# Fused attention and feed-forward kernel: the loads of seven token chunks, each cut into two transfers

## The chip, the cores and the metric

The kernel runs on one core of a Trainium2 chip. The metric is the device time of one execution in microseconds (us). The kernel before takes 298.97 us, the median of three runs (298.57, 298.97 and 299.29 us).

A core has TensorE (PE, matrix products, with a row PEld for its weight loads), VectorE (DVE), ScalarE (ACT), GpSimd (POOL) and SyncE (SP). They run side by side, each with its own queue of instructions, and wait for one another through semaphores. Sixteen DMA engines move data between the main memory (HBM) and the on-chip memory (SBUF). In this kernel POOL issues all loads but two, and SP issues the stores and the transposing DMAs.

## The reference, cut to what matters

```
q, k, v: (8 batches, 8 heads, 576 tokens, 64) float32; w_in (512, 2048), w_out (2048, 512)

scores = (q @ k.T) / sqrt(64)
Dmat   = gamma[h] ** (i - j) where i >= j, else 0      # gamma[h] = 1 - 2**(-5 - h)
x      = (scores * Dmat) @ v                           # heads side by side: (4608, 512)
h      = x @ w_in
out    = (h * tanh(softplus(h))) @ w_out               # (4608, 512) float32
```

## The kernel before, in words

The 4608 tokens are cut into 36 chunks of 128. Chunks 0 to 7 are the first 128 tokens of each batch. Then come, for each pair of batches, three chunks of each batch and one chunk that holds the last 64 tokens of both: chunks 8 to 10 and 11 to 13 belong to batches 0 and 1, chunk 14 is their shared rest, 15 to 17 and 18 to 20 belong to batches 2 and 3, 21 is their shared rest, and so on. Four chunks form a feed-forward tile, so there are nine tiles.

Attention is done chunk by chunk with a running state for each batch (`total`). For a chunk n from 8 on the steps are these:

- `load(n)` (line 267) issues the loads of q, k and v, each 128 tokens by 8 heads by 64, 256 KB, on POOL's queue (line 276). A shared chunk has two loads of 64 tokens for each of the three (line 283). q and k go to the halves of one buffer, `qkraw`, of which there are five; v goes to `vraw`, of which there are seven.
- `step_p(n)` scales q and k on DVE (`qks`, line 295), two instructions for a chunk. `step_v(n)` scales v (`vs`, line 302), on DVE up to chunk 19 and on POOL after it.
- `step_t(n)` transposes q and k: for chunks up to 15 on TensorE (line 316), from chunk 16 on by a transposing DMA that SP issues (line 324, `qkT`).
- `visit(n)` handles two chunks on TensorE: the states of the next pair (line 393), the outputs of this pair (lines 452 and 469) and the scores of the next pair (line 338). It ends with two copies out of PSUM to the transposed activations `xT` (line 481), one on ACT and one on DVE.

The feed-forward products (line 518; line 523 is the same in two halves) fill TensorE between the visits: `g1` writes to one of two PSUM banks called `hp` and ACT applies the activation (line 547), `g2` sums into `ops`, and line 599 copies the result out for the store. The two `xT` copies read the same two `hp` banks, so `g1` cannot go on in a bank before its copy is done.

The order of all work is written out by hand. The loads of chunks 8 to 11 are issued in a row (line 661). Those of chunks 12 to 16 are issued in the loop over u (line 708), and those of 17, 18 and 19 wait for an activation of the third tile (line 512, `gated`). From chunk 20 on `hold(n)` (line 485) comes first: a one-column copy on POOL that reads the transposed `qkT` of chunk n. POOL works in order, so the loads behind it are not issued before that transposing DMA has landed. `hold(16)` stands before the load of chunk 20, and `hold(18)` before that of chunk 21. `load_k0(b)` (line 257) loads 256 KB of k once more for the states.

In the trace the DMAs that POOL issues carry eight semaphores in turn, and each issue waits for the semaphore that it will use: it waits until the DMA issued eight before it on POOL's queue has landed. The code does not say this; the framework does it.

Of the kernel before, what the change touches and what calls it, by code (L numbers as in the profile page):

```python
# [16 lines left out]
def kernel(  # L17
# [18 lines left out]
    nc = tc.nc  # L36
    B, H, S, D = q.shape
    assert (B, H, S, D) == (8, 8, 576, 64)
    P = 128
# [227 lines left out]
    def load(n, gate=None):  # L267
        if n >= n_chunks:
            return
        b, c = chunks[n]  # L270
        qkr = io.tile([P, 2, H, D], F32, name="qkraw")
        vr = io.tile([P, H, D], F32, name="vraw", bufs=7)
        live[n] = {"qkr": qkr, "v": vr}
        for t, src in ((qkr[:, 0], q), (qkr[:, 1], k), (vr, v)):
            if c < 4:
                ins = nc.gpsimd.dma_start(  # L276
                    out=t, in_=src[b, :, ds(P * c, P), :].rearrange("h p d -> p h d"))
                if gate is not None:
                    behind(ins, gate)
                    gate = None  # L280
            else:
                for e in range(2):
                    nc.gpsimd.dma_start(
                        out=t[ds(64 * e, 64)],
                        in_=src[b + e, :, ds(512, 64), :].rearrange("h p d -> p h d"))
# [76 lines left out]
    def behind(ins, others):  # L362

        sync = mybir.DependencyInfo(mybir.DependencyClass.Sync, mybir.DependencyReason.DATA)
        tc.add_manual_dep(ins.ins, others.ins.name, sync, reason="row halves and a bank")
# [168 lines left out]
    def g1(t, f, parts=1, begun=None):  # L534
        if t not in gts:
            gts[t] = gp.tile([P, nF, NCH * P], BF16, name="gT")
        if begun is not None:
            hp = begun
        elif (t, f) == (0, 2):
            hp = ps_o.tile([P, NCH * P], F32, name="ops")  # L540
        else:
            hp = ps_h.tile([P, NCH * P], F32, name="hp")
        n = NCH * P // parts
        for j in range(0 if begun is None else 1, parts):
            for c in range(KC):
                product(hp[:, ts(j, n)], w_in_t[:, c, ts(f, P)], xts[t][:, c, ts(j, n)], c == 0, c == KC - 1)
        done = nc.scalar.activation(gts[t][:, f, :], hp, AX.Mish)  # L547
        if (t, f) in gated:
            load(gated[t, f], done)
            queued[0] += 1  # L550
# [110 lines left out]
    for b in range(4):  # L661
        load(N0 + b)
        if b == 0:
            load_k0(0)
# [13 lines left out]
    for i in range(nF):  # L678
        for step in steps.get(i, "").split():
            n = int(step[1])  # L680
# [17 lines left out]
    def more_loads(upto):  # L698
        for _ in range(2):
            if queued[0] <= upto:  # L700
                load(queued[0])
                queued[0] += 1
# [55 lines left out]
    for t in range(2, nT + 1):  # L758
        for i in range(nF):
            n, w = NCH * (t + 1) + i // 8 * 2, i % 8  # L760
# [104 lines left out]
```

## Time and profile before

| | |
|---|---|
| median of three runs | 298.97 us |
| the profiled execution's own time | 298.96 us |
| its span (first to last instruction) | 297.3 us |
| PE busy | 288.0 us (97%) |
| DVE, ACT, POOL busy | 136.7, 133.0, 128.5 us |
| moved by DMA | 47.97 MB, mean 161 GB/s |
| POOL's own DMA queue (q0) | 32.25 MB, 50.6% of the 16 engines' span |
| granted TensorE clock | 1.0 throughout |

The profile is that of one execution. An instruction's line gives its start, its duration, the engine, the line of the kernel, the operation, and what it writes and reads (out<-in). In brackets stands the time that the engine sat idle before it and who ended that wait. "To landing" is the time from the issue of a DMA to the moment when all its data are there. Times are counted from the start of the span.

### The profile page before, as it was taken

Reading aid. Unit: us, or ns where it says so; the run is one execution under the profiler, and the core shown is the slowest. Engines: PE = TensorE matmul, PEld = TensorE weight load, DVE = VectorE, ACT = ScalarE, POOL = GpSimd, SP = SyncE. Lnnn points to the kernel's source line nnn. Section 1 sums busy time; section 2 is a strip of 40 time slices with the busy share of each in tenths; the row PEclk is TensorE's granted clock in tenths of the full one; section 3 lists DMA queues with packets and bytes.
Section 4 is the critical chain, followed back from the end, with each engine's and each line's share of the span. In section 5 each row is a group of like instructions: output and inputs, shape, how many; then the busy total and the mean of one; then the engine's idle time right before and its main releaser. Section 6 shows DMA issues by size and latency. Waiting matters only on the chain.

```text
span 297.3 us, 7902 instructions
## 1 busy us (share of the span) xinstructions
PE 288.0 (97%) x3444; PEld 157.4 (53%) x3482; DVE 136.7 (46%) x241; ACT 133.0 (45%) x219; POOL 128.5 (43%) x170
## 2 busy tenths in 40 slices
PE   8999998999999999999999999999999999999996
PEld 3566886555556545456645454545454544444443
DVE  3841546598858727453546453535354222010011
ACT  5667225876656544434363435343444333433200
POOL 8845665767662279294658547283020000000000
PEclk9999999999999999999999999999999999999999
DMA  7999999999999979998989988685414110110131
GB/s 149 208 202 205 204 239 217 337 237 191 273 239 180 197 164 223 196 218 188 237 165 228 176 217 213 140 206 142 87 45 98 37 37 35 37 35 35 53 91 71
DMA packets 42259, 47.97 MB, mean 161 GB/s; under 512 B 23920, under 2 KB 31088, under 8 KB 42224
## 3 DMA queue, kind: packets, MB, share of 16 engines
q0 software_dynamic: 15424, 32.25, 50.6%
q1 hardware_dynamic: 26656, 15.01, 22.2%
q8 instruction: 27, 0.44, 0.6%
q10 hardware_dynamic: 144, 0.20, 0.2%
q14 instruction: 8, 0.07, 0.1%
HBM read 38.80 MB, written 9.44 MB: 162 GB/s over the span
## 4 chain that ended last, share of the span: by engine, by line
PE 81%; DMA 12%; POOL 3%; issue 2%; DVE 1%; POOLq 0%; DVEq 0%
PE hp L518 38%; PE ops L518 30%; DMA vpair<-in_v_dram 5%; DMA w_out_t<-in_moe_w_out_dram 4%; DMA w_in_t<-in_moe_w_in_dram 3%; PE hp L523 2%; PE ops L523 2%; PE sc L338 1%; PE sc L393 1%; PE hp L469 1%; PE hp L452 1%; PE hp L591 1%; POOL gT L107 1%; PE sc L316 1%; POOL gT L118 1%
## 5 line engine op out<-in xcount | busy, mean ns | idle before, releaser
L518 PE MATMUL hp<-xT,w_in_t 128*128 128x512 bf16 (+1 forms) x507 | 126.3, 376 | 1.3 <-DVE xT L249 0.6
L547 ACT ACTIVATE gT<-hp 128x512 bf16<-128x512 f32 x143 | 85.4, 598 | 93.0 <-PE hp L518 87.1
L518 PE MATMUL ops<-w_out_t,gT 128*128 128x512 bf16 x410 | 101.6, 379 | 2.0 <-issue 1.9
L518 PEld LDWEIGHTS <-w_in_t 128*128 128x128 bf16 x528 | 51.3, 98 | 54.1 <-issue 0.8
L518 PEld LDWEIGHTS <-gT 128*128 128x128 bf16 x478 | 45.5, 98 | 52.2
L599 DVE COPY res<-ops 128x512 f32<-128x512 f32 x28 | 19.3, 691 | 90.7 <-PE ops L518 90.7
L295 DVE TENSOR_TENSOR qks<-qkraw,gqk 128x512 bf16<-128x512 f32 x56 | 35.3, 685 | 5.3 <-DMA qkraw<-in_k_dram 5.3
L276 POOL DMA_DIRECT2D qkraw<-in_q_dram x24 | 21.7, 904 | 8.3 <-DMA vpair<-in_v_dram 2.7
L487 POOL COPY held<-qkT 128x1 bf16<-128x1 bf16 x10 | 2.6, 264 | 51.3 <-DMA qkT<-qks 51.3
L302 POOL TENSOR_TENSOR vs<-vraw,gv 128x512 bf16<-128x512 f32 x16 | 16.4, 1045 | 15.1 <-PE hp L452 15.0
L276 POOL DMA_DIRECT2D vraw<-in_v_dram x24 | 21.2, 884 | 2.7 <-DMA vpair<-in_v_dram 1.5
L276 POOL DMA_DIRECT2D qkraw<-in_k_dram x24 | 21.3, 888 | 1.7 <-DMA w_out_t<-in_moe_w_out_dram 1.0
L481 DVE CAST xT<-hp 128x512 bf16<-128x512 f32 x13 | 9.0, 691 | 25.8 <-PE hp L469 25.8
L481 ACT CAST xT<-hp 128x512 bf16<-128x512 f32 x14 | 8.2, 586 | 28.1 <-PE hp L469 28.1
L523 PEld LDWEIGHTS <-gT 128*128 128x128 bf16 x164 | 15.7, 98 | 3.2
L429 DVE TENSOR_TENSOR total<-sc,total 128x256 f32<-128x256 f32 x40 | 16.9, 422 | 1.0
L344 DVE TENSOR_TENSOR sm<-sc,mask 128x1024 bf16<-128x1024 f32 x14 | 17.0, 1216 | 0.7 <-PE sc L338 0.7
L523 PE MATMUL hp<-xT,w_in_t 128*128 128x256 bf16 x102 | 15.7, 273 | 0.0
L523 PEld LDWEIGHTS <-w_in_t 128*128 128x128 bf16 x104 | 10.2, 98 | 6.7
L432 ACT CAST ssb<-total 128x768 bf16<-128x768 f32 (+3 forms) x13 | 11.7, 897 | 1.7 <-DVE total L429 1.6
L518 PE MATMUL hp<-w_out_t,gT 128*128 128x512 bf16 x49 | 12.0, 379 | 0.2 <-issue 0.2
L523 PE MATMUL ops<-w_out_t,gT 128*128 128x256 bf16 x80 | 10.4, 273 | 0.2
(123 smaller groups left out, 250.4 us busy)
## 6 DMA issues: line engine op xcount, KB each, us to landing
out_dram<-res SPq DMA_DIRECT2D x31, 256.0 KB, 3.2
qkraw<-in_q_dram POOLq DMA_DIRECT2D x24, 256.0 KB, 6.3
qkraw<-in_k_dram POOLq DMA_DIRECT2D x24, 256.0 KB, 6.5
vraw<-in_v_dram POOLq DMA_DIRECT2D x24, 256.0 KB, 6.8
w_out_t<-in_moe_w_out_dram POOLq DMA_DIRECT2D x4, 512.0 KB, 11.9
k0r<-in_k_dram POOLq DMA_DIRECT2D x8, 256.0 KB, 7.5
gT<-in_k_dram POOLq DMA_DIRECT2D x8, 128.0 KB, 6.6
gT<-in_v_dram POOLq DMA_DIRECT2D x2, 512.0 KB, 7.2
```

Source lines behind the costliest of these rows:

```text
L107: nc.gpsimd.dma_start(out=fst[t][name][:, b, :], in_=(q, k)[i][4 * t + b, :, 0:P, :].rearrange("h (g r) d -> g h (r d)", r=8))
L276: ins = nc.gpsimd.dma_start(out=t, in_=src[b, :, ds(P * c, P), :].rearrange("h p d -> p h d"))
L295: nc.vector.tensor_tensor(slots[:, :, y], heads[:, :, y], factors[:, :, y].unsqueeze(3).to_broadcast([P, NP, 2, D]), op=OP.mult)
L302: engine.tensor_tensor(vs, live[n]["v"], gv[:, c, :].unsqueeze(2).to_broadcast([P, H, D]), op=OP.mult)
L344: nc.vector.tensor_tensor(sm.rearrange("p e x n i -> p (e x n) i"), live[n]["sc"].rearrange("p e x n i -> p (e x n) i"), mask.unsqueeze(1) ...
L429: nc.vector.tensor_tensor(new[:, k], st[:, j, x], total[b], op=OP.add)
L432: casts.append(lambda copy: copy(lows[:, 0:k], new[:, 0:k]))
L481: copy(xts[t][:, :, ds(P * s, 2 * P)].rearrange("p h (x j i) -> p j h x i", x=2, j=2)[:, j], both[j])
L518: newest[0] = nc.tensor.matmul(to, lhsT=w, rhs=x, start=first, stop=last)
L523: nc.tensor.matmul(to[:, ts(j, n)], lhsT=w, rhs=x[:, ts(j, n)], start=False, stop=False, skip_group_check=True)
L547: done = nc.scalar.activation(gts[t][:, f, :], hp, AX.Mish)
L599: copy(ot, ops)
```

## The change

Each load of q, k and v of chunks 10 to 13 is issued as two DMAs, the first 112 tokens and then the last 16. Each load of chunks 15 to 17 is issued as two DMAs of 80 and 48 tokens. That is 21 loads and so 21 more DMAs on POOL's queue. Bytes, buffers and the order of everything else stay. Chunk 14, the shared rest, was already loaded in halves of 64 tokens. The `gate` (the wait for an activation, chunk 17 among the seven) goes to the first DMA of a chunk.

```diff
         for t, src in ((qkr[:, 0], q), (qkr[:, 1], k), (vr, v)):
             if c < 4:
-                ins = nc.gpsimd.dma_start(
-                    out=t, in_=src[b, :, ds(P * c, P), :].rearrange("h p d -> p h d"))
-                if gate is not None:
-                    behind(ins, gate)
-                    gate = None
+                first_part = 112 if 10 <= n < 14 else 80 if 14 < n < 18 else P
+                for p0, np_ in ((0, first_part), (first_part, P - first_part)):
+                    if np_ == 0:
+                        continue
+                    ins = nc.gpsimd.dma_start(
+                        out=t[ds(p0, np_)], in_=src[b, :, ds(P * c + p0, np_), :].rearrange("h p d -> p h d"))
+                    if gate is not None:
+                        behind(ins, gate)
+                        gate = None
             else:
```

## The prediction

> **What bounds the kernel now.** I read the page first, then the busy time by stretches, then POOL's timeline, then the waits and timelines of DVE and PE around the places where a late load would be felt.
>
> ```profile
> span 297.3 us, 7902 instructions
> PE 288.0 (97%) x3444; PEld 157.4 (53%) x3482; DVE 136.7 (46%) x241; ACT 133.0 (45%) x219; POOL 128.5 (43%) x170
> DMA  7999999999999979998989988685414110110131
> ...
> 50.00:75.00 25.00, 24.71 (x494) 14.85 (x494) 18.17 (x32) 17.92 (x31) 17.71 (x23) 1.00 1.03 253
> 75.00:100.00 25.00, 24.42 (x400) 14.33 (x392) 18.06 (x30) 14.29 (x23) 13.58 (x16) 1.00 0.98 227
> 125.00:295.00 170.00, 167.39 (x1857) 84.55 (x1876) 61.78 (x102) 63.66 (x105) 52.77 (x66) 1.00 0.51 124
> ```
>
> The columns of the last three lines are the stretch, its length, the busy time of PE, PEld, DVE, ACT and POOL, the granted clock, the share of the DMA engines and GB/s. From 50 us on PE is busy 24.71 and 24.42 of 25 us at full clock, so there is nearly nothing to win there: of the first stretch 0.3 us is idle, of the second 0.6. The DMA engines are full (1.03, 0.98) until about 94 us, and half empty afterwards. The execution took 298.96 us, 1.66 more than its span; the median of the three runs is 298.97, so I count from 298.96. About 0.2%, 0.6 us, is what a measurement of this kernel can tell from no change.
>
> ```profile
> 46.81 1.12 POOL L276 DMA_DIRECT2D qkraw<-in_q_dram  x1 [2.68 <-DMA vpair<-in_v_dram]
> 48.02 0.88 POOL L276 DMA_DIRECT2D qkraw<-in_k_dram  x1
> 49.21 0.88 POOL L276 DMA_DIRECT2D vraw<-in_v_dram  x1 [0.31 <-DMA qkraw<-in_k_dram]
> ...
> 62.32 0.70 POOL L283 DMA_DIRECT2D qkraw<-in_q_dram  x1 [0.61 <-DVE total L429]
> ...
> 94.61 0.73 POOL L487 COPY held<-qkT 128x1 bf16<-128x1 bf16 x1 [7.98 <-DMA qkT<-qks]
> 95.29 0.89 POOL L276 DMA_DIRECT2D qkraw<-in_q_dram  x1
> ...
> 105.81 0.19 POOL L487 COPY held<-qkT 128x1 bf16<-128x1 bf16 x1 [7.01 <-DMA qkT<-qks]
> 106.33 1.37 POOL L283 DMA_DIRECT2D qkraw<-in_q_dram  x2 [0.34 <-issue]
> ```
>
> The first three lines load chunk 10, the first changed one. The waits named by a DMA are the ring of eight semaphores: k of chunk 10 goes out 0.29 us after q of chunk 8 landed (47.73), eight DMAs earlier. Afterwards the two `hold` copies end long waits for transposing DMAs; what the loads of chunks 20 and 21 wait for is a landing, not POOL.
>
> ```profile
> 111.83 1.29 DVE L295 TENSOR_TENSOR qks<-qkraw,gqk 128x512 bf16<-128x512 f32 x2 [1.75 <-DMA qkraw<-in_k_dram]
> 113.04 0.69 DVE L255 TENSOR_TENSOR v0s<-vpair,gv 128x512 bf16<-128x512 f32 x1
> 113.64 0.69 DVE L481 CAST xT<-hp 128x512 bf16<-128x512 f32 x1
> ...
> 113.79 1.89 PE L518 MATMUL hp<-xT,w_in_t 128*128 128x512 bf16 x8
> ```
>
> This is the tightest place. DVE waits for k of chunk 21, and behind that step it has the copy that frees a bank `hp`: done at 114.33. PE's fifth of these eight products, the first in that bank, starts at 114.65. A late chunk 21 has 0.3 us before PE stands.
>
> **POOL: 21 more issues.** An issue of 128 tokens takes 0.88 us, one of 64 tokens 0.69: 0.19 for 64 tokens. On that line 112, 16, 80 and 48 tokens take 0.83, 0.55, 0.74 and 0.64, so each cut load takes 1.38 instead of 0.88: 21 x 0.50 = 10.5 us more on POOL. It is covered by POOL's waits for the ring and by DMA work already queued. I walked the ring with three rules from the rows: an issue begins 0.28 us after the landing eight before, or when POOL is free; a landing is no sooner than 1.57 us plus its transfer after the issue's end (half-load at 106.33: 2.9 to landing, less 0.69, less 0.64); whole loads land 1.20 apart. On the kernel before this gives 58.0 for v of chunk 10 (58.1 in the trace) and 70.0 for v of 13 (70.7). With the change the ring holds four loads instead of eight and POOL runs late: v of 13 begins to go out at 66.9 instead of 60.8, v of 19 at 89 instead of 85.8. Both still go out over 3 us before the engines come to them, so POOL itself delays nothing. If that cover is gone, because a landing needs 3 us after its issue and not 1.57, the walk ends 0.9 us later than with the price below.
>
> **The DMA engines: 21 more completions and smaller pieces.** No row shows a piece of 16, 48, 80 or 112 tokens. The nearest is chunk 14, in halves of 64: its six landings lie 3.82 us apart in all (70.73 to 74.55), 1.27 for a pair against 1.20 for a whole load, 0.07 more. By the rate it is dearer: 193 GB/s between 70.8 and 74.4 against 216 between 63 and 69, which is 1.36 against 1.21 for 256 KB, 0.15 more. At the low end a second completion costs next to nothing: 0.01. A gain I exclude, since the bytes are the same and the engines already full. I take 0.07, for landings are what the next step waits for. The lag then grows to 0.14 us at k of chunk 10, 0.35 at 11, 0.56 at 12, 0.77 at 13 and 21 x 0.07 = 1.5 at the end of the backlog, v of chunk 19 (landed at 93.6).
>
> **Who feels the lag, up to 100 us.** Chunk 10: DVE already waits for k (57.04), and the 1.0 us that it idles before 59.94 takes up 0.14. Chunk 11: k lands 60.5, used 62.11. Chunk 12: 65.5, used 66.11, and 0.66 us of idle DVE follows; lag 0.56. Chunk 13: k 69.4 and v 70.7, used 71.11 and 72.92; lag 0.8. Chunk 15: 78.7, used 79.90; lag 1.0. Chunk 16: 81.8, used 82.31, late by some 0.7, hidden by 3.2 us of idle DVE before 86.82. Chunk 17: 86.4, used 89.16. None reaches PE. The transposing DMAs of chunks 16 and 17 (88.70 and 91.82, landing at 94.5 and 96.0) end when the loads ahead of them are through, so they move by up to 1.5; PE takes chunk 17's result at 97.80, 1.7 us after it landed. SP issues nothing more, and its order stays.
>
> **Who feels it after that.** `hold(16)` is released by the first of these DMAs. Behind it in POOL's queue stand the loads of chunk 20 and a k0 load (landing 103.3), which share the engines with the transposing DMA of chunk 18 (100.40 to 105.7; alone such a DMA takes 3.2 us, at 190.96). That releases `hold(18)`, and behind it come the loads of chunk 21, whose k DVE already waits for. Each link passes the lag on, so the step at 111.83 moves by 1.5 us, the copy with it, and PE stands 1.5 - 0.3 = 1.2 us at 114.65. PE has no idle time later in which to win it back. The v steps on POOL behind those loads (116.55) are not needed until the visit at 127. The sum: 298.96 + 1.2 = 300.2 us, 0.4% slower.
>
> **Rivals.** First, no change: the second completion costs 0.01 (lag 0.2), or the idle time of the DMA engines between the links (their share is 0.08 from 95.5 to 97 us and 0.21 from 106.5 to 108) takes most of 1.5 us up. Then at most 0.5 us reach PE: 298.9 to 299.5. For it speaks that the transposing DMA of chunk 16 has 5.8 us of which only the end lies in the backlog; against it, that every link is released by a landing. The point from which it decides is a lag of 0.9 us at 111.83.
>
> [...]
>
> [...]
>
> Third, faster: shorter queues could bring the transposing DMAs and stores through earlier. There is 0.9 us of idle PE between 50 and 100 us, most of it fixed pauses of 0.2 to 0.3 us after the visits, so even half of it gives 298.5, not 0.2%.
>
> **How the numbers follow.** The chain of lags has 50%: 300.2, within 299.6 and 301.0 (prices from 0.04 to 0.11). Slow small pieces have 12%: 301.6. No change has 33%: 298.9 to 299.5. Faster by over 0.2% is left 5%. So faster 0.05, same 0.33, slower 0.62. The range from 298.8 to 301.6 leaves out the faster case and the upper half of the second rival.
>
> **What would show it.** Right: POOL's issues of 16 tokens near 0.55 us; k of chunk 13 landing about 0.8 later and v of 19 about 1.5 later; both `hold` copies later by more than 1 us while PE is still on time; the wait of DVE for k of chunk 21 grown, and PE idle before a product into `hp` near 115. Wrong: `hold(18)` at 105.8 as before, or PE standing earlier, at 70 to 75 us, where the pieces would have to cost over 0.15 each.

## The result and the profile after

The changed kernel takes 307.45 us, the median of four runs (306.90 to 308.62); the kernel before takes 299.10 us beside it (298.57 to 299.29). The ratio is 1.0285, with a 95% interval of 1.0249 to 1.0321: 8.3 us slower, where 1.2 us was forecast and 301.6 us was the upper end. In several kernels below single executions scatter by 3 to 10 us; medians and ranges are those of all executions, while a ratio leaves out those over 1.5% above the fastest of their kernel, and so can lie nearer to 1 than the medians do.

The profiled execution of the changed kernel took 306.90 us, 7.94 more than the one shown of before. First the page's head, then the busy time by stretches (the columns are those of the prediction).

```profile
span 305.2 us, 7937 instructions
...
PE 288.9 (95%) x3444; PEld 157.7 (52%) x3482; DVE 137.7 (45%) x241; ACT 133.0 (44%) x219; POOL 138.2 (45%) x191
...
PEclk9999999999999799999999999999999999999999
DMA  7999999998989789999997978968504110110032
```

```profile
50.00:75.00 25.00, 24.18 (x490) 14.40 (x490) 17.74 (x31) 17.70 (x31) 21.72 (x32) 1.00 0.93 243
75.00:100.00 25.00, 22.65 (x340) 13.21 (x332) 15.62 (x26) 13.70 (x22) 19.49 (x27) 1.00 0.97 210
100.00:125.00 25.00, 22.23 (x280) 11.12 (x284) 14.85 (x25) 9.57 (x16) 12.46 (x16) 0.93 0.89 175
125.00:150.00 25.00, 23.07 (x310) 13.36 (x311) 10.66 (x17) 9.82 (x16) 14.11 (x17) 1.00 1.05 165
```

POOL is busy 9.7 us longer, as forecast (10.5). But PE is idle 2.4 and 2.8 us between 75 and 125 (0.6 and 0.3 before), and 1.9 more before 150, and for a while its clock is not granted in full: 0.93 on average between 100 and 125, where it was 1.00 before. PE's own timeline says where, the line of before first:

```profile
97.80 0.45 PE L338 MATMUL sc<-qkT 64*64 64x64 bf16 x32
```

```profile
97.76 0.32 PE L342 MATMUL sc<-qkT 64*64 64x64 bf16 x16
102.22 0.43 PE L342 MATMUL sc<-qkT 64*64 64x64 bf16 x16 [4.15 <-DMA qkT<-qks]
...
148.00 0.34 PE L342 MATMUL sc<-qkT 64*64 64x64 bf16 x16
150.60 0.32 PE L342 MATMUL sc<-qkT 64*64 64x64 bf16 x16 [2.27 <-DMA qkT<-qks]
```

Both stalls are scores that wait for a transposing DMA: that of chunk 17 at 98 us, that of chunk 23 at 148. The first puts PE 4.3 us behind the trace of before. The clock is granted at half for 3.4 us around its end, which costs 1.2 more. The second adds 2.4. The sum is 7.9, the whole difference. (At 72.4 us PE also waits 0.45 for DVE, which had waited 1.13 for k of chunk 12; but this execution had been 0.6 us ahead until then.)

So the question is why chunk 17's transposing DMA lands at 102.18 instead of 96.03. It was issued at 91.82 before and at 90.73 after; the last number is the time to landing, before and after:

```profile
qkT<-qks SPq DMA_TRANSPOSE x1, 4.2
```

```profile
qkT<-qks SPq DMA_TRANSPOSE x1, 11.4
```

POOL's timeline, two lines of before and then the changed kernel:

```profile
81.38 0.88 POOL L276 DMA_DIRECT2D qkraw<-in_q_dram  x1
...
85.75 0.88 POOL L276 DMA_DIRECT2D vraw<-in_v_dram  x1
```

```profile
46.23 1.74 POOL L280 DMA_DIRECT2D qkraw<-in_q_dram  x2 [1.43 <-DMA vpair<-in_v_dram]
48.64 0.83 POOL L280 DMA_DIRECT2D qkraw<-in_k_dram  x1 [0.67 <-DMA qkraw<-in_k_dram]
49.83 0.53 POOL L280 DMA_DIRECT2D qkraw<-in_k_dram  x1 [0.36 <-DMA vraw<-in_v_dram]
...
86.80 0.89 POOL L280 DMA_DIRECT2D qkraw<-in_q_dram  x1 [0.91 <-DVE qks L299]
...
91.18 0.88 POOL L280 DMA_DIRECT2D vraw<-in_v_dram  x1
94.69 0.19 POOL L491 COPY held<-qkT 128x1 bf16<-128x1 bf16 x1 [2.63 <-DMA qkT<-qks]
95.22 0.89 POOL L280 DMA_DIRECT2D qkraw<-in_q_dram  x1 [0.34 <-issue]
...
111.24 0.19 POOL L491 COPY held<-qkT 128x1 bf16<-128x1 bf16 x1 [12.51 <-DMA qkT<-qks]
```

112 tokens take 0.83 us to issue and 16 take 0.53. The waits for the ring of eight semaphores are there as before, but each now covers half as many bytes. From 57 us on POOL hardly rests. The loads of chunk 18 begin to go out at 86.80 (81.38 before), and v of 19, the last before the `hold`, at 91.18 (85.75 before), 5.4 us late. The stretches of both kernels show what that does, first before, then after:

```profile
57.00:70.00 13.00, 12.79 (x284) 7.20 (x285) 11.13 (x20) 8.70 (x17) 7.78 (x11) 1.00 1.05 246
...
80.00:93.00 13.00, 12.79 (x195) 7.06 (x196) 9.71 (x17) 8.28 (x13) 6.63 (x8) 1.00 1.08 228
```

```profile
57.00:70.00 13.00, 12.68 (x288) 7.29 (x289) 11.24 (x20) 8.35 (x16) 12.59 (x19) 1.00 0.93 225
...
80.00:93.00 13.00, 12.79 (x195) 7.07 (x196) 9.95 (x17) 8.24 (x14) 11.15 (x15) 1.00 0.86 200
```

POOL is idle 0.4 us of the first stretch instead of 5.2, and the DMA engines, always full before (1.05, 1.08), stand at 0.93 and 0.86: they run dry while POOL is still issuing. The work that they did not do then is done later, at the same time as the transposing DMAs. The DMA queues show it (q1 carries SP's DMAs, q0 POOL's; the columns are packets, MB and the share of the 16 engines). Before, from 94.4 to 96.0 us:

```profile
DMA packets 1074, 0.27 MB, mean 167 GB/s; under 512 B 1072, under 2 KB 1072, under 8 KB 1074
q1 hardware_dynamic: 1074, 0.27, 74.3%
```

After, from 96.0 to 100.6:

```profile
DMA packets 1207, 0.78 MB, mean 169 GB/s; under 512 B 1074, under 2 KB 1074, under 8 KB 1207
q0 software_dynamic: 143, 0.48, 65.8%
q1 hardware_dynamic: 1064, 0.29, 49.6%
```

A transposing DMA is about a thousand packets of 256 bytes. Before, chunk 17's go through once the last load is in, with q0 empty, in about 1 us. After, the same thousand take 4.6 us, for 143 packets of loads, of 4 KB mostly, run between them. Neither queue waits here for the other to be empty: some seven packets of q1 go through for one of q0 (1064 against 143).

### The profile page after: what moved, and what is told of

It reads as the page before. It is cut to its first block, busy times and chain, and to the rows that moved or that the text cites. A ratio compares the mean times of both kernels' runs of the same rounds, so it can differ in the third digit from the quotient of the medians.

```text
span 305.2 us, 7937 instructions
## 1 busy us (share of the span) xinstructions
PE 288.9 (95%) x3444; PEld 157.7 (52%) x3482; DVE 137.7 (45%) x241; ACT 133.0 (44%) x219; POOL 138.2 (45%) x191
## 4 chain that ended last, share of the span: by engine, by line
PE 68%; DMA 22%; DVE 3%; POOL 3%; issue 3%; DVEq 0%; POOLq 0%
PE hp L522 31%; PE ops L522 28%; DMA qkT<-qks 8%; DMA qkraw<-in_k_dram 5%; DMA w_out_t<-in_moe_w_out_dram 4%; DMA gT<-in_v_dram 3%; DMA qkraw<-in_q_dram 2%; POOL gT L107 1%; DVE qks L299 1%; PE sc L342 1%; PE hp L473 1%; PE hp L595 1%; PE hp L527 1%; PE sc L397 1%; PE hp L456 1%
## 5 line engine op out<-in xcount | busy, mean ns | idle before, releaser
L280 POOL DMA_DIRECT2D qkraw<-in_q_dram x31 | 25.4, 821 | 6.1 <-issue 1.8
L280 POOL DMA_DIRECT2D qkraw<-in_k_dram x31 | 24.8, 800 | 2.7 <-DMA w_out_t<-in_moe_w_out_dram 0.9
L280 POOL DMA_DIRECT2D vraw<-in_v_dram x31 | 24.5, 793 | 2.6 <-DMA vpair<-in_v_dram 1.5
L527 PEld LDWEIGHTS <-w_in_t 128*128 128x128 bf16 x104 | 10.2, 98 | 6.6
L342 PE MATMUL sc<-qkT 64*64 64x64 bf16 x448 | 7.1, 198 | 6.4 <-DMA qkT<-qks 6.4
```

The source lines that it names most:

```text
L280: ins = nc.gpsimd.dma_start(out=t[ds(p0, np_)], in_=src[b, :, ds(P * c + p0, np_), :].rearrange("h p d -> p h d"))
L342: nc.tensor.matmul(sc[i, e, x, p, :], lhsT=qk[r, 1, p, i], rhs=qk[r, 0, p, i], start=True, stop=True, skip_group_check=True)
L527: nc.tensor.matmul(to[:, ts(j, n)], lhsT=w, rhs=x[:, ts(j, n)], start=False, stop=False, skip_group_check=True)
```

## The experiments

### One part of the change alone

```diff
-first_part = 112 if 10 <= n < 14 else 80 if 14 < n < 18 else P
+first_part = 112 if 10 <= n < 14 else P
```

> Only chunks 10 to 13 are cut (112 and 16 tokens, 12 more DMAs, 6 us more on POOL). Theory A, POOL's issue time: POOL falls behind by up to 6 us at chunk 13, but the loads of 15 and 16 are whole, so it catches up before the load of chunk 17, which waits for its activation until 78.8 us anyway; chunks 18 and 19 go out as in the kernel before, the second transposing DMA (chunk 17) lands near 96 us, and the time is 298.5 to 299.8. Theory C, slow small pieces: the 16-token pieces are the worst of all, so most of the loss is here: 304 to 307.

```diff
-first_part = 112 if 10 <= n < 14 else 80 if 14 < n < 18 else P
+first_part = 80 if 14 < n < 18 else P
```

> Only chunks 15 to 17 are cut (80 and 48 tokens, 9 more DMAs, 4.5 us more on POOL). Theory A: POOL reaches chunk 18 some 2 us later than before (83.5 instead of 81.4) and ends chunk 19 near 89 instead of 86.6, so that these loads run into the two transposing DMAs of chunks 16 and 17; PE waits at the scores of chunk 16 for part of what the full change loses: 300 to 305. Theory C: 48 and 80 tokens are slower by little: 299 to 300.

The first group alone takes 302.97 us (298.94 to 305.05), ratio 1.0038 with an interval of 0.9983 to 1.0093; the second alone 302.05 us (298.77 to 304.43), ratio 1.0067 (1.0023 to 1.0111); the kernel before 299.44 beside them. By the medians either part costs some 3 us; by the ratios it is 0.4% and 0.7%, and the first interval holds no change at all. The median of the first lies in neither of the two ranges expected for it. Neither shows the stall at the scores in its trace, but that of the second is of its shortest execution (298.77 us), so what its longer ones lose can't be seen. POOL catches up in both: v of chunk 19 begins to go out at 87.36 and 88.40. The profiled execution of the first is one of its longer ones (304.06 us). In it PE stands at the place that the prediction named. DVE there, and PE:

```profile
114.67 1.29 DVE L299 TENSOR_TENSOR qks<-qkraw,gqk 128x512 bf16<-128x512 f32 x2 [4.32 <-DMA qkraw<-in_k_dram]
115.88 1.53 DVE L255 TENSOR_TENSOR v0s<-vpair,gv 128x512 bf16<-128x512 f32 x1
117.34 0.68 DVE L485 CAST xT<-hp 128x512 bf16<-128x512 f32 x1
```

```profile
114.07 1.03 PE L522 MATMUL hp<-xT,w_in_t 128*128 128x512 bf16 x4
118.07 1.73 PE L522 MATMUL hp<-xT,w_in_t 128*128 128x512 bf16 x4 [2.97 <-DVE xT L485]
```

The step that waits for k of chunk 21 begins 2.8 us later than before (111.83), and PE goes on 3.4 us later than before (114.65). In that execution the chain of lags is real, then, and larger than 1.2 us: v of 19 lands 2.1 us late (95.69 against 93.58), and a v0 step between the two, 0.69 us before, takes 1.53 here.

### POOL's time, and places in the ring

Both kernels leave the loads of before whole. The first adds a write of a junk tile behind each of the 21 loads (0.52 us on POOL, no DMA). The second adds a tiny DMA there, of 16 rows of 8 numbers into a junk tile: it shows 0.52 us on POOL too, and takes a place in the ring as well. All outputs are still computed.

```diff
+                if 10 <= n < 14 or 14 < n < 18:
+                    nc.gpsimd.memset(junk, 0.0)                     # junk: 128 x 480 bf16
```

> The kernel before, all loads whole, but behind each of the 21 loads of chunks 10 to 13 and 15 to 17 stands a memset on POOL (128 x 480 bf16, estimated 0.4 to 0.6 us from the 0.17 us of the 64-column memset) that nobody reads. No DMA and no semaphore of the ring is added. Theory A (issue time alone): POOL begins chunk 18 near 85 to 87 us, the transposing DMA of chunk 17 lands near 100 to 102 and the time is 303 to 308. Theory B (the ring of eight, with half as many bytes in flight) and theory C (the pieces on the DMA engines) both expect 298.7 to 300, since neither is touched.

```diff
+                if 10 <= n < 14 or 14 < n < 18:
+                    nc.gpsimd.dma_start(out=junk.pop(),
+                        in_=src[b, 0:1, ds(P * c + 112, 16), 0:8].rearrange("h p d -> p h d"))
```

> The kernel before, all loads whole, but behind each of the 21 loads stands a further DMA of 16 x 8 numbers into a place that nobody reads: the same 21 more issues on POOL (about 0.5 us each) and the same 21 more places of the ring, with next to no bytes and no load cut. Theory A: as the full change, 303 to 308. Theory B: likewise 303 to 308, but with the memset run at 299. Theory C: 298.7 to 300.

With POOL's time alone: 304.02 us (299.71 to 309.18), ratio 1.0048 (0.9991 to 1.0106). With the places in the ring as well: 308.76 us (307.51 to 311.01), ratio 1.0298 (1.0247 to 1.0349), as much as the change. No load was cut in either, so a loss of this size needs no small pieces. The median of the first lies in the range of the theory of POOL's time (303 to 308), but not by its mechanism: chunk 17's transposing DMA was to land near 100 to 102 and landed at 97.18, and the trace (303.77 us) has its stall at the tight place instead. Their stretches, POOL's time alone first:

```profile
46.00:57.00 11.00, 10.90 (x103) 7.46 (x100) 6.46 (x10) 8.76 (x16) 10.83 (x16) 1.00 1.04 270
...
80.00:93.00 13.00, 12.79 (x198) 7.24 (x199) 9.79 (x18) 8.24 (x14) 8.74 (x12) 1.00 1.01 224
```

```profile
46.00:57.00 11.00, 10.88 (x109) 7.58 (x109) 6.59 (x11) 8.26 (x15) 6.53 (x9) 1.00 1.03 263
...
80.00:93.00 13.00, 12.79 (x195) 7.05 (x196) 8.69 (x15) 7.76 (x13) 12.55 (x18) 1.00 0.87 196
```

The memsets run in the waits for the ring: POOL is idle 0.17 us of 46 to 57, and it has caught up by the end (4.3 us idle from 80 to 93). The tiny DMAs cannot do that: they too stand in the ring, so POOL stays idle 4.5 us of 46 to 57, falls behind, and works 12.55 of the last 13 us. Then v of 19 begins to go out at 92.76 instead of 87.86, chunk 17's transposing DMA lands at 107.46 instead of 97.18, and PE stands 9.2 us at the scores. This is what the ring does in the change too (POOL busy 7.00 of 46 to 57).

The two kernels are not equal in POOL's time, though: from one load to the next it is 1.31 us with a memset and 1.43 with a tiny DMA. From the first load of chunk 10 to v of 19 the second takes 4.1 us more, of which 2.4 is POOL's own work and 1.7 is waiting. The change is the better partner of the memsets: it takes 3.2 us more than they do, 0.9 of it work and 2.3 waiting.

### The last six loads late, and nothing else

The loads of before, with 4 or 10 junk writes on POOL ahead of the load of chunk 18: 2.2 and 5.5 us.

```diff
+        if n == 18:
+            for _ in range(10):        # 4 in the first kernel
+                nc.gpsimd.memset(junk, 0.0)
```

> The kernel before with four memsets on POOL (0.52 us each, 2.1 us) directly before the loads of chunk 18; nothing else differs, no load is cut, and chunks 10 to 17 go out as before. Theory, late loads of 18 and 19 are the whole cause: the last load goes out near 88 instead of 85.8 us, the transposing DMAs land 1 to 2 us later, chunk 21 is late, and PE stands at 114.7: 300 to 304, as with the first group alone. Rival, the late chunks 10 to 17 do the harm: 298.5 to 299.8.

> The same with ten memsets, 5.2 us: chunk 18 goes out at 86.6 us and chunk 19 ends at 91.9, as in the full change (86.8 and 92.1). Theory: the second transposing DMA lands after 100, PE stands near 98 us, and the time is that of the full change, 305 to 309. Rival, chunks 10 to 17: 298.5 to 299.8.

2.2 us: 301.75 us (298.37 to 308.93), ratio 1.0049 (1.0006 to 1.0092), the kernel before 298.70 beside both; its trace is of one of the longer ones (303.06 us). 5.5 us: 307.84 us (305.81 to 308.68), ratio 1.0288 (1.0235 to 1.0341), the change's own ratio. POOL and PE in the second:

```profile
81.08 5.50 POOL L272 MEMSET junk<- 128x480 bf16 x10
...
90.99 0.88 POOL L279 DMA_DIRECT2D vraw<-in_v_dram  x1
```

```profile
97.44 0.32 PE L341 MATMUL sc<-qkT 64*64 64x64 bf16 x16
102.24 0.43 PE L341 MATMUL sc<-qkT 64*64 64x64 bf16 x16 [4.49 <-DMA qkT<-qks]
```

v of 19 goes out at 90.99 (changed kernel 91.18), and PE resumes at 102.24 (102.22). With no load cut, six late loads make the whole loss. At 2.2 us the scores are on time and PE stands at the tight place instead, 2.14 us before 117.08.

### What holds the transposing DMA

Two loads could be beside it: those of chunk 20, which `hold(16)` lets out at 95.22, or the late ones of 18 and 19. The first kernel is the changed one with chunk 20 behind a later transposing DMA (chunk 17's), the second the changed one with the load of chunk 19 no longer ahead of `hold(16)` but behind it.

```diff
-                hold(n + 4)
+                hold(n + 5 if n + 4 == NT else n + 4)
```

> The full change, but the copy that holds the loads of chunk 20 back waits for the second transposing DMA (chunk 17) and not for the first. Theory, load 20 is what slows that DMA: in the full change it began its packets at 96 us, just when the loads of chunk 20 came in; without them it lands near 98 to 99 instead of 102.2, PE stands 0.5 to 1.5 us at the scores of chunk 16 instead of 4.3, part of the gain is lost again because the loads of chunk 20 go out 3 us later, and the time is 301 to 305. Rival, the late loads of chunks 18 and 19 alone hold it up: it still lands after 101 and the time stays at 306 to 309.

```diff
-    gated = {(2, 0): 17, (2, 1): 18, (2, 3): 19}
+    gated = {(2, 0): 17, (2, 1): 18}
```

> The full change, but the loads of chunk 19 stand behind the copy that waits for the first transposing DMA, so that of the late loads only those of chunk 18 are in the DMA engines beside the second one. If the late loads in flight hold that DMA up, it lands at 96 to 98.5 us instead of 102.2 and PE stands at most 0.5 us at the scores of chunk 16; the late chunk 19 then blocks DVE before the copy out of the visit, so that PE stands there for 1 to 3 us and the time is 301 to 307. If the second DMA is slow for another reason, it lands after 101 as before.

Chunk 20 later: 306.68 us (306.47 to 310.27), ratio 1.0299 (1.0225 to 1.0374), nothing gained. Its first load goes out at 102.31, when chunk 17's transposing DMA has landed already, and that still lands only at 101.64; PE resumes the scores at 101.69. So chunk 20 is not what holds it.

Chunk 19 later: chunk 17's transposing DMA lands at 95.79, 4.2 us after its issue, and the stall at the scores is gone. PE in this kernel:

```profile
98.35 0.45 PE L342 MATMUL sc<-qkT 64*64 64x64 bf16 x32
...
102.18 2.75 PE L522 MATMUL hp<-xT,w_in_t 128*128 128x512 bf16 x12 [1.26 <-DVE xT L485]
```

That settles the place: it is the loads still in flight, chunk 19's above all. As a remedy it is poor. The profiled execution took 302.44 us, the ratio is 1.0070 (1.0027 to 1.0112), but seven of the ten executions took 304.7 to 307.5 and the median is 306.13 (before 298.78). What those lose is not in a trace, for the profile is of one of the others; there PE waits for DVE at 100 us, and 1.4 us more for chunk 23's transposing DMA.

### The size of the pieces, and another engine to issue them

All seven chunks in halves of 64 tokens; and the change with its second pieces issued by ACT.

```diff
-first_part = 112 if 10 <= n < 14 else 80 if 14 < n < 18 else P
+first_part = 64 if 10 <= n < 14 or 14 < n < 18 else P
```

> The same seven chunks cut in the middle, 64 and 64 tokens: the same 21 more issues and ring places, other sizes. If the number of issues and ring places decides, the time is that of the full change, 306 to 309. If the small and uneven pieces decide, it is nearer to the kernel before, 299 to 303.

```diff
-                    ins = nc.gpsimd.dma_start(
+                    ins = (nc.scalar if p0 else nc.gpsimd).dma_start(
```

> The full change, but the second pieces (16 and 48 tokens) are issued by ACT, so that POOL has one issue and one place of its ring for each load, as before, while the DMA engines move the same pieces. If POOL's issue time and ring are the cause, POOL begins chunk 18 near 81 us again, PE does not stand at the scores of chunk 16, and the time is 298.5 to 301 (ACT pays 21 issues of some 0.4 us, which may cost a few tenths). If the pieces on the DMA engines are the cause, 305 to 309.

Halves take 306.30 us, the median of four executions: three took 305.95 to 308.57 and one 299.98. In the profiled one (306.65) chunk 17's transposing DMA lands at 104.14 and PE stands 6.3 us. So even pieces lose as much as uneven ones, in three executions of four. Together with the tiny DMAs beside whole loads this says that the number of DMAs counts, and not how a load is cut. The 8 us of the change come from the issuing queue: tiny DMAs beside whole loads took 308.76 us with no load cut.

With pieces on ACT: 305.45 us (304.27 to 305.64), ratio 1.0205 (1.0158 to 1.0252), where I expected most of the loss to be gone. The stall at the scores is indeed gone, and the transposing DMAs land 3.6 and 3.1 us after their issue. But POOL did not begin chunk 18 near 81 us, as expected: it waits 5.9 us for an ACT result before chunk 17 and begins 18 at 85.33. ACT itself now waits for landings (1.9 us) and issues the pieces, and PE is idle 5.2 us from 40 to 93 us (1.7 before), 2.3 of it in waits for ACT (0.4 before). Another 2.1 us were lost before 40 us, ahead of every cut load. One loss took the place of another, so this run neither supports nor weakens the account.

### The tight place at 114.65

The first group alone with DVE's step for chunk 21 moved behind the `xT` copy, and the kernel before with the same move. In the first two changes of the diff chunk 21's step joins a rule that was there for chunk 17; the third takes its transposing DMA out of the old place, so that it is issued once, right behind the moved step.

```diff
-            if w in ((4, 7) if n + 4 == NT else (4, 5)) and n + 4 >= NT:
+            if w in ((4, 7) if n + 4 in (NT, NT + 4) else (4, 5)) and n + 4 >= NT:
...
-            if w == 7 and n + 4 == NT:
+            if w == 7 and n + 4 in (NT, NT + 4):
...
-                    for x in (4, 5):
+                    for x in ((4,) if n + 4 == NT + 4 else (4, 5)):
```

> Chunks 10 to 13 cut as in the first-group run, and on DVE the scaling of chunk 21 moved behind the copy that frees the bank for PE (its transposing DMA stays where it was on SP). If the stall at 114.7 us comes by that order (late k of chunk 21, then the copy, then PE), it is gone and the time falls from 303 to 298.5 to 300.0, unless the later DMA of chunk 21 is missed at the visit at 127 us. If PE stands there for another reason, 302 to 304 as before.

> The kernel before with the scaling of chunk 21 behind the copy that frees the bank, as in the run with the moved DVE step, and nothing cut. The kernel before has 0.3 us to spare at that place in its profile, so in an execution like that one nothing is won: 298.3 to 299.3. Where the loads come late by chance the step may stand in the way as well; then the scatter of the times narrows towards 298.5.

With the move, the first group takes 301.39 us (299.98 to 309.20), ratio 1.0071 (1.0026 to 1.0116), against a median of 302.97 without it, on another chip. That is above the 298.5 to 300.0 expected, and still 2.7 us above the kernel before beside it (298.70). In its trace (300.99 us) the stall is gone: of PE's waits between 90 and 125 us only one group is left (the answer gives the time in total, how often, and the longest).

```profile
PE ops L522 <- issue: 0.3, 2, 0.2
```

But PE is 2.0 us late from 49 us on in that execution, before any cut load is needed, so the two times can't be set against each other closely. The kernel before with the move takes 298.64 us (297.77 to 300.12), ratio 1.0001 (0.9973 to 1.0029): no change, and no version here beats the kernel before.

### The runs side by side

One execution of each, by its trace (80/48 alone by its shortest of ten, 112/16 alone and late by 2.2 by longer ones): when v of chunk 19 begins to go out on POOL, the share of the DMA engines from 80 to 93 us, when chunk 17's transposing DMA lands, and PE's longest idle time from 90 to 125 us.

| kernel | v of 19 out | DMA share | transposing DMA 17 | PE stands |
|---|---|---|---|---|
| before | 85.75 | 1.08 | 96.03 | no |
| 112/16 alone | 87.36 | 1.04 | 98.20 | 2.97 at 118.07 |
| POOL's time alone | 87.86 | 1.01 | 97.18 | 3.63 at 117.95 |
| late by 2.2 | 88.14 | 1.01 | 97.14 | 2.14 at 117.08 |
| 80/48 alone | 88.40 | 0.99 | 97.15 | no |
| late by 5.5 | 90.99 | 0.84 | 102.20 | 4.49 at 102.24 |
| the change | 91.18 | 0.86 | 102.18 | 4.15 at 102.22 |
| chunk 20 later | 91.33 | 0.89 | 101.64 | 3.44 at 101.69 |
| halves | 91.47 | 0.82 | 104.14 | 6.30 at 104.18 |
| places in the ring | 92.76 | 0.87 | 107.46 | 9.18 at 107.51 |

Up to 88.4 the transposing DMA moves by some 1 to 2 us, about as the prediction had it. From 91.0 on it moves by 5.6 and more. In between lies its own issue, between 90.6 and 92.0 us in all these kernels but not far apart: loads issued well ahead of it are through in time, and loads issued beside it share the engines with it to the end.

## Why the prediction was wrong

**What held.** PE is full and had nothing to win. POOL's price was right (0.83, 0.53, 0.73 and 0.63 us an issue against 0.83, 0.55, 0.74 and 0.64), and so was the ring up to chunk 13: v of 13 goes out at 66.83, where the walk had 66.9. The direction came out right, but by another path than the forecast one. The rival of slow small pieces fell as the cause of the loss: whole loads with tiny DMAs beside them cost as much as the change, and halves nearly so. No run shows the term behind its 301.6 us, the time that a small piece takes on the engines; in its place the runs showed 308.76 us with no load cut and 306.30 with even halves. The tight place at 114.65 is one: it stops PE in the traces of four kernels, and in the one trace with DVE's step moved the stall is gone.

**What agreed by luck.** v of chunk 17 lands 1.4 us later (88.98 against 87.59), where 0.07 for each of 21 loads makes 1.5. But it went out 4.0 us later (84.54 against 80.50), to engines that were partly idle, so this is no measure of the price of a cut load. The other landings do not follow 0.07 at all: k of chunks 10 to 13 lands 0.0, 0.9, 1.2 and 0.3 us later, where 0.14, 0.35, 0.56 and 0.77 were forecast, and v of 19, with 1.5 forecast, lands 8.4 us later (101.93 against 93.58). No run shows the price by itself.

**The step that failed: "Both still go out over 3 us before the engines come to them, so POOL itself delays nothing."** The walk had v of 19 going out at 89; the trace has 91.18. Half of that is the sum: from 66.9 on, v of 13, six halves, a k0 load, nine cut loads and five whole ones take 23.2 us by the prediction's own prices, so it had to say 90.1 even with no wait between. The rest is mostly waits, of which the profile puts 0.91 us, before q of 18, down to DVE. Worse, there was no cover. The engines' share fell to 0.86 from 80 to 93 us: they had come to the end of what was issued. The rule that a landing is 1.57 us plus the transfer after the issue's end was short as well: q of 18 lands 3.0 us after its issue ended (2.8 by the rule), and a piece of 48 tokens of v of 17 3.1 us after (2.0 by the rule). A longer landing stood in the prediction ("needs 3 us"), but priced at 0.9 us, because only the end of the loads was asked for.

**And with it: the transposing DMAs "move by up to 1.5".** They were treated as standing at the end of one line, so that they would be late by as much as the line. They are not in that line: they share the engines with whatever loads are there. With v of 19 out at 88.4 or before, chunk 17's moved by 1 to 2 us; with it out at 91, chunk 17's thousand packets go between packets of 4 KB and land 6.2 us late. With 1.8 us of slack at 97.80 that is 4.4 us of PE, and 4.3 were lost. The rows showed that the load queue was empty when the packets of before went through; I read it as an order, not as a gap that had to stay clear.

**The chain after it** did not come to pass in the changed kernel in the form forecast. `hold(16)` begins only 0.1 us later (94.69), and `hold(18)` 5.4 us later (111.24), as late as PE itself, which has slid by 5.5: measured from PE it is on time. DVE's step for chunk 21 still waits for its k (1.42 us, 1.75 before), at 117.02, with PE as late as it. The chain shows up only where the first stall does not, or is shorter (chunk 20 later, where PE stands at both places). Of the named signs of being wrong one came true: PE stood at 72.4 us, for 0.45 us, after DVE had waited 1.13 us for k of chunk 12 (landed at 66.69 instead of 65.46).

**What was not in the sum at all**: the half clock behind a stall (1.2 us), and the second stall at 148 us (2.4). Chunk 23's transposing DMA took 13.8 us (8.3 before), beside a v and a k0 load that took 12.9 each. That it is the same contention is argued from these rows; no run took it out.

**What stays open.** The change's lateness comes from POOL's time and from places in the ring. From the first load of chunk 10 to v of 19 POOL works 10.2 us more than before and waits only 4.2 us less, where with the memsets it works 9.3 more and waits 6.5 less. How much of that difference is the ring and how much the wait for DVE was not separated. The price of a cut load on the engines is open. Why the executions of several kernels lie several us apart is open too.

## What to carry to other kernels

When a queue of loads covers an engine that issues them, ask two things of the cover: how many bytes it is (eight places in a ring are half the bytes once each load is two DMAs; here the DMA engines' share from 80 to 93 us fell from 1.08 to 0.86), and what else needs the engines just when it ends. A transfer that slips through a gap between loads, as chunk 17's transposing DMA did here (4.2 us from issue to landing in the gap, 11.4 beside loads), sets those loads a deadline, even if no instruction says so: read from the queues whether it ran alone, and price the loss of the gap and not only the lag. Then ask what a busy PE loses behind its first stall, for here that was more than a quarter of the stall again (1.2 us behind one of 4.3).

## What the runs showed of the hardware beside that

- **The clock after a stall.** With the granted clock by stretches, the time at half clock comes out as 3.4 us with PE's stalls of 4.15 us (the change), 2.97, 3.63 and 2.14 us, and as 6.8 us with 4.49 and 6.30 us, 10.2 us with 9.18 (each is twice the clock missing, summed over the stretches). After a stall of 1.26 us it stayed at 1.00, and so it did after the change's own second stall, of 2.27 us. In the kernel that is late by 2.2 us:

```profile
114.00:115.00 1.00, 0.94 (x5) 0.31 (x4) 1.00 (x3) 0.02 (x1) 1.00 (x2) 1.00 1.05 229
...
116.00:117.00 1.00, 0.00 (x0) 0.00 (x0) 1.00 (x3) 0.00 (x0) 1.00 (x2) 1.00 1.07 229
...
118.00:119.00 1.00, 1.00 (x5) 0.40 (x4) 0.16 (x1) 0.60 (x1) 1.00 (x2) 0.63 2.36 185
...
120.00:121.00 1.00, 1.00 (x3) 0.30 (x2) 0.97 (x3) 0.00 (x0) 0.00 (x0) 0.50 1.03 83
```

  Here the clock (third column from the end) falls 1.2 us after PE is back at work (118.27 against 117.08); in the change it falls 0.6 us before (101.64 against 102.22). The three lengths, 3.4, 6.8 and 10.2 us, are multiples of 3.4. The length of a stall alone does not decide: 2.14 us of idle PE sufficed here, the 2.27 us of the change's second stall did not, and neither did a stall of 1.9 us in the kernel with chunk 20 later (the mean clock of that execution, 0.993, leaves room for one time of 3.4 us at half clock, that of its stall of 3.44 us, and not for a second). Why 2.14 us did and 2.27 did not, no run shows.
- **A transposing DMA beside loads** took 10.8 to 15.5 us from issue to landing (chunk 17's, in the last five rows of the table), where it took 4.2 before and, at 190.96 us of the kernel before, 3.2 alone.
- **A scaling step on DVE** (v0, 128x512) took 1.53 us instead of 0.69 in four traces (112/16 alone, POOL's time alone, late by 2.2, chunk 20 later), but 0.69 in the change and late by 5.5, where chunk 21 was late too. POOL was issuing loads beside it in both kinds. Why was not tried.
